# One load for K's weights, one load for each pair of last weight rows, and tile 3's transposes ahead of K2's second pass

## The chip, the cores and the metric

The program runs on one core of a Trainium2 chip. The metric is the device time of one execution in microseconds (us); a run's figure is the median of several executions. A separate execution was profiled, and its trace is what the views below are taken from.

## What is computed

The input `x` has 2048 rows (tokens) of 576 values. It is normalised, goes through a linear-attention block with 32 heads of 18 values and through a GEGLU feed-forward block of width 4608, and both results are added to `x`:

```python
xn  = layernorm(x)
q, k, v = split(xn @ wqkv)                 # wqkv: 576 x 1728, heads of 18
pq, pk  = phi(q), phi(k)                   # phi(t) = (t+1 if t>0 else exp(t)) + 1e-6
kv = sum_s pk[s] v[s]^T ;  z = sum_s pk[s]
A  = ((pq @ kv) / (pq . z + 1e-6)) @ wo
B  = (gelu(xn @ w_gate) * (xn @ w_up)) @ w_down
out = x + A + B                            # all inputs and the output in bf16
```

## The kernel before

**Tiling.** The 2048 tokens are 16 tiles of 128 (tile n holds every sixteenth token). The 576 columns are five contraction tiles: four of 128 and a last one of 64. To use all of TensorE's rows for the odd 64, a matrix product is done as "row tiles": each matmul uses only 64 of the 128 contraction rows, two run side by side on the two halves (`LO` = partitions 0 to 63, `HI` = 64 to 127), and each writes to a PSUM bank of its own. A product (`_Unit`, line 242) therefore has two passes. In the first (`rows`, line 258, often called p1 here) `LO` works for bank 0 and `HI` for bank 1; in the second (`p2`, line 271) they change places. Between them stands a "turn", a no-op on GpSimd (POOL) that makes the second pass wait for the first.

**The tokens of the head.** `_Token` (line 434) makes K or Q of one tile: its 576 output columns are two halves of 288, one for each bank. Its first pass has contraction tiles 0 to 3 (8 matmuls), its second has tiles 0 to 4 (10 matmuls). Contraction tile 4, the last 64 rows of the weights, is read from `w_ends`: one half of the columns lies in partitions 0 to 63 and the other half in 64 to 127, so that each half has the last rows where its second pass works.

**The weight loads.** `load_w_main` (line 167) brings rows 0 to 511 of K's or Q's weights, or some of its four contraction tiles. `load_w_ends` (line 172) brings the last 64 rows with two loads of 64 partitions x 576 bytes. The start of the kernel (lines 207 to 218) issues on SyncE's queue (SP): tile 0 of x, K's weights in two parts (contraction tiles 0 and 1, then 2 and 3, `W_PARTS`), tile 2 of x, Q's weights in two parts, tile 3 of x, and Q's ends. Tile 1 of x is issued by ScalarE (ACT), K's ends by POOL.

**What keeps TensorE (PE) busy before data is there.** `spin` (line 228) issues 31 matmuls of 128 x 128 on a tile `warm` that VectorE (DVE) sets to zero (line 210). `row_spin` issues eight more between the transposes of tile 0 and tile 1.

**Normalising.** Tiles 0 and 1 are handled as "centred" tiles: only the mean is subtracted before K and Q are computed, and the results are scaled afterwards. Tiles 2 and 3 are normalised first. Each of the four goes through PE transposes (line 358, PSUM banks from `tp_banks`, tile 3 in banks 2 and 3) and two copies to SBUF, one by ACT and one by DVE (line 363). Later tiles are transposed by DMA (line 366).

**The order.** The order on PE is written by hand (line 490):

```python
line = "t0 t1 K0a K0b K1 . . Q0a Q1a Q0b Q1b t2 u1 . . K2 Q2 . t3 . K3 Q3 .".split()
```

`t` and `u` are a tile's transposes, a name such as `K1` is its first pass, `K0a` and `K0b` are the halves of a first pass that go with the two parts of the weights, and a "." is the second pass of the oldest product that still lacks it. Thus `K2 Q2 . t3 . K3` reads: first passes of K2 and Q2, second pass of K2, transposes of tile 3, second pass of Q2, first pass of K3. After that the raw gate/up products (`g`) alternate with the other K tiles. The other engines' orders come from `in_order` (line 70), a planner that plays all steps with costs and ready times written into the code (`X_AT`, `W_AT`, `ready=`) and emits them in the order of its simulated starts. SP's later loads follow a fixed list (line 606). After the head come the Gram matrix of `xn` and `pk`, the attention state, the gate/up products in four blocks of 512 tokens, and the down products.

Of the kernel before, what the change touches and what calls it, by code (L numbers as in the profile page):

```python
# [10 lines left out]
BF16 = mybir.dt.bfloat16  # L11
F32 = mybir.dt.float32
PSUM = bass.MemoryType.PSUM

P = 128
HP = 64
S = 2048
D = 576
# [8 lines left out]
HALF = D // 2  # L27
# [5 lines left out]
EPS_LN = 1e-5  # L33
# [1 line left out]
GUB = 2  # L35
NB = NF // GUB
NWBUF = 4
NWARM = 31
XW = D + HP
RAW = 14  # L40
PK0 = 18
# [4 lines left out]
HEAD_T = RAW_T + ("Q2",)  # L46
LATER = 40.0
CENTRED = (0, 1)
W_PARTS = ((0, 1), (2, 3))
LEAD = 5  # L50


# [37 lines left out]
def kernel(  # L90
# [11 lines left out]
    nc = tc.nc  # L102
# [8 lines left out]
    const = ctx.enter_context(tc.tile_pool(name="const", bufs=1))  # L111
# [5 lines left out]
    ps_all = psum.tile([P, 8, 512], F32, name="ps_all")  # L117
# [4 lines left out]
    LO, HI = slice(0, HP), slice(HP, P)  # L122
# [7 lines left out]
    xnT = persist.tile([P, KT, S], BF16, name="xnT")  # L130
# [24 lines left out]
    wqkv_sb = apool.tile([P, KT, 3 * D], BF16, name="wqkv_sb")  # L155
    xn = apool.tile([P, NS, XW], BF16, name="xn")
    xcT = apool.tile([P, KT, len(CENTRED) * P], BF16, name="xcT")
    w_ends = apool.tile([P, 2, HALF], BF16, name="w_ends")
# [5 lines left out]
    def load_x(n0, cnt, on=nc.sync):  # L164
        on.dma_start(x_sb[:, n0:n0 + cnt, 0:D], x_view[:, n0:n0 + cnt, :])  # L165

    def load_w_main(which, kts=slice(0, 4)):
        c = slice(which * D, (which + 1) * D)
        view = A_wqkv[0:4 * P, c].rearrange("(kt p) c -> p kt c", p=P)
        nc.sync.dma_start(wqkv_sb[:, kts, c], view[:, kts, :])  # L170

    def load_w_ends(which, on):
        for i, rows in enumerate((HI, LO)):
            c = which * D + i * HALF
            on.dma_start(w_ends[rows, which, :], A_wqkv[512:576, c:c + HALF])

    def load_w_last(which, rows):
        c = slice(which * D, (which + 1) * D)
# [4 lines left out]
    def load_ends(i, on=nc.sync, parts=(0, 1)):  # L183
        c = slice(GUB * P * (i % NB), GUB * P * (i % NB + 2))
        if parts[0] == 0:
            wr_pairs[i // 2] = wr_bufs.next()
        for part in parts:
            on.dma_start(wr_pairs[i // 2][(LO, HI)[part], :], (B_w_gate, B_w_up)[part][512:576, c])

    def load_gu(i, part):  # L190

        if i >= NSC * NB:
            return
        f0 = GUB * (i % NB)
        c0, c1 = f0 * P, (f0 + GUB) * P
        if part == 0:
            gu_blocks[i] = (wg_bufs.next(), wu_bufs.next())
            if i % 2 == 0 and i:
                load_ends(i)
            nc.sync.dma_start(gu_blocks[i][0][:], B_w_gate[0:512, c0:c1].rearrange("(kt p) c -> p kt c", p=P))  # L200
        else:
            nc.sync.dma_start(gu_blocks[i][1][:], B_w_up[0:512, c0:c1].rearrange("(kt p) c -> p kt c", p=P))
# [3 lines left out]

    load_x(0, 1)
    nc.scalar.preload_act_table_set("natural_log_exp_and_others")
    warm = const.tile([P, P], BF16, name="warm")
    nc.vector.memset(warm[:], 0.0)  # L210
    nc.vector.memset(x_sb[:, 1, 0:1], 0.0)
    load_x(1, 1, nc.scalar)
    load_w_ends(1, nc.gpsimd)
    for which in (1, 0):
        for kts in W_PARTS:
            load_w_main(which, slice(kts[0], kts[-1] + 1))
        load_x(3 - which, 1)
    load_w_ends(0, nc.sync)

    act_bias = const.tile([P, 1], F32, name="act_bias")  # L220
    eps_ln = const.tile([P, 1], F32, name="eps_ln")
    nc.vector.memset(eps_ln[:], EPS_LN)
    ident = const.tile([P, P], BF16, name="ident")
    make_identity(nc, ident[:])
    bmask = const.tile([P, CR], F32, name="bmask")
# [2 lines left out]
    def spin(count):  # L228

        for _ in range(count):  # L230
            nc.tensor.matmul(ps_all[:, 7, 0:P], lhsT=warm[:], rhs=warm[:], start=True, stop=True)

    def row_spin(count):

# [3 lines left out]

    spin(NWARM)

# [125 lines left out]
        nc.sync.dma_start_transpose(xnT[:, :, n * P:(n + 1) * P], xn[:, n, :])  # L366

    X_AT = [3.46, 3.86, 6.40, 8.70]
    W_AT = {"K": (5.00, 5.70), "Q": (7.50, 8.50)}
    DMA_FREE = 8.9  # L370

    places = {}
# [11 lines left out]
    for n in range(NS):  # L384
# [26 lines left out]
        ready = [("rstd", n if n < 6 else both), twin]  # L411
# [3 lines left out]
        on, took = ("ACT", 0.92) if NORM[n] == "A" else ("DVE", 0.45)  # L415
# [18 lines left out]
    class _Token:  # L434

        def __init__(self, kind, n, ring=banks):
            self.kind, self.n, self.c = kind, n, (D if kind == "K" else 0)
            self.banks = two_banks(ring)
            self.unit = _Unit(
                [ps_all[:, b, :HALF] for b in self.banks], lambda i, rows, kt: (xcT if n in CENTRED else xnT)[rows, kt, n * P:(n + 1) * P],  # L440
                self.weights, nc.gpsimd, first=range(KT - 1), then=range(KT),
            )
            self.acc = ps_all[:, self.banks[0]:self.banks[0] + 2, :HALF]

        def weights(self, i, rows, kt):
            if kt == 4:
                return w_ends[rows, self.c // D, :]
            return wqkv_sb[rows, kt, self.c + i * HALF:self.c + (i + 1) * HALF]

        def raw(self):  # L450
            dst = (pk if self.kind == "K" else pq)[:, self.n, :].rearrange("p (h c) -> p h c", h=2)
# [35 lines left out]
                out=hT[:, self.f:self.f + NF + 1:NF, :], in_=ps_all[:, self.two[0]:self.two[0] + 2, :],  # L487
            )

    line = "t0 t1 K0a K0b K1 . . Q0a Q1a Q0b Q1b t2 u1 . . K2 Q2 . t3 . K3 Q3 .".split()  # L490
    follow = [f"g{i}" for i in range(LEAD)]
    for i in range(12):
        follow += [f"K{i + 4}"] + ([f"g{i + LEAD}"] if i + LEAD < RAW else [])
# [10 lines left out]
    def pe(name, took, after, call, ready=0.0):  # L504
        if name in steps:
            s = steps[name]
            s.after = s.after + ([pe_prev[0]] if pe_prev[0] else [])
        else:
            step(name, "PE", took, 0, after + ([pe_prev[0]] if pe_prev[0] else []), call, ready=ready, tail=0.17)
        pe_prev[0] = name  # L510
# [4 lines left out]
    for b in range(RAW // GUB):  # L515
        for part in range(2):
            war = [("p2", f"g{2 * (b - 4) + 1}")] if b > 4 else [("p2", "g1")] if b == 4 else []
            war += [(("gu", b, 0), "q")] if part else [(("gu", b - 1, 1), "q")] if b else []
            load(("gu", b, part), 0.6 + 1.1 * (b % 2 == 0 and part == 0 and b > 0), 262 + 131 * (b % 2 == 0 and part == 0 and b > 0), 6.8 + 6.0 * (b - 1), war,
                 lambda b=b, part=part: load_gu(b, part), ready=5.4, count=1 + 2 * (b % 2 == 0 and part == 0 and b > 0))  # L520

    def p2_step(u):
        n = int(u.name[1:])
# [16 lines left out]
    for name in line:  # L540
        if name == ".":
            p2_step(pending.pop(0))
            continue
        kind, n = name[0], int(name[1:].rstrip("ab"))
        if kind == "u":
            pe(("tu", n), 0, [], None)
            owner[(tp_banks[2], tp_banks[2] + 1)] += [("xnU", n, 0), ("xnU", n, 1)]
            continue
        if kind == "t":
            two = (tp_banks[n], tp_banks[n] + 1)  # L550
            steps[("tp", n)].after = steps[("tp", n)].after + owner.get(two, [])
            pe(("tp", n), 0, [], None)
            owner[two] = [("xnT", n, 0), ("xnT", n, 1)]
            if name == "t0":
                pe("spin", 0.22, [], lambda: row_spin(4))
            continue
        if name[-1] == "b":
            u = pending[-1 if name[:2] == pending[-1].name else -2]
            pe(("p1", u.name), 0.245, [], lambda u=u: u.p1(W_PARTS[1]), ready=W_AT[kind][1])
            step(("turn", u.name), "POOL", 0.06, clock, [("p1", u.name)], u.swap, tail=0.05)  # L560
            continue
        u = _Chain()
        u.name, u.at = name[:2] if name[-1] == "a" else name, clock
        if kind in "KQ":
            u.body = _Token(kind, n, head_banks if u.name in HEAD_T else banks)
            b = u.body.banks
            after = [("xnT", n)]
            t1, u.t2 = 0.49, 0.615
            u.p1 = u.body.unit.rows
            u.swap = u.body.unit.swap  # L570
            u.unit_p2 = u.body.unit.p2
            at = W_AT[kind][0 if name[-1] == "a" else -1]
        else:
            u.body = _Raw(n)
            b = u.body.two
            blk = n // GUB
            after = [("xnU" if m in CENTRED else "xnT", m) for m in range(TPC)] + [("gu", blk, i) for i in range(2)] + [("ends", 0), ("ends", 1)] * (blk == 0)
            t1, u.t2 = 1.08, 0.865
            u.p1 = u.body.rows
            u.swap = lambda body=u.body: body.unit.swap()  # L580
            u.unit_p2 = lambda body=u.body: body.unit.p2()
            at = 0.0
        after += owner.get(tuple(b), [])
        clock += t1 + u.t2
        if name[-1] == "a":
            pe(("p1a", u.name), 0.245, after, lambda u=u: u.p1(W_PARTS[0]), ready=at)
        else:
            pe(("p1", name), t1, after, u.p1, ready=at)
            step(("turn", name), "POOL", 0.06, u.at, [("p1", name)], u.swap, tail=0.05)
        pending.append(u)  # L590
# [372 lines left out]
    for sc in range(NSC):  # L963
# [15 lines left out]
        for j, t in enumerate(tiles):  # L979
            u = t.unit()  # L980
# [45 lines left out]
```

## Time and profile before

| | us |
|---|---|
| median of 3 runs | 506.54 (506.53 to 506.62) |
| the profiled execution's own time | 506.81 |
| span of its trace (first to last instruction) | 505.1 |
| PE busy | 500.3 (99%) |
| DVE, ACT, POOL busy | 230.1, 152.1, 10.5 |
| DMA queue q1 (all loads that SP issues) | 113802 packets, 60.54 MB |
| granted TensorE clock | 1.00 in every stretch |

How to read the views: the timeline lists, in order of time, the start, the length and the engine of merged instructions, and in brackets how long the engine stood idle before and what ended that. "PEld" is the load of the stationary operand, which overlaps the matmuls. An engine's name with a q ("SPq", "POOLq") is its queue while it issues a DMA. The chain of waits follows the work that ended last back to the start. In the list of DMA queues the columns are packets, MB, and the time that the packets took as a share of 16 DMA engines over the window asked for; q1 carries what SP issues, q10 what ACT issues, q0 what POOL issues.

Issues on SP at the start, from the timeline: x tile 0 at 0.81, the two parts of K's weights at 1.27 (0.93 us for both), x tile 2 at 2.24, the two parts of Q's weights at 2.75 (0.94), x tile 3 at 3.74, the two loads of Q's ends at 4.25 (1.26), the first gate load at 5.56.

### The profile page before, as it was taken

How to read it: one execution, taken by the hardware profiler on the slowest of the kernel's cores; microseconds unless marked ns; L12 is line 12 of the kernel's file. 1: busy time of each engine (PE TensorE's matmuls, PEld its weight loads, DVE VectorE, ACT ScalarE, POOL GpSimd, SP SyncE). 2: the span in 40 equal slices, each digit the busy share in tenths (PEclk: the TensorE clock that was granted, in tenths of full speed). 3: DMA queues.
4: the chain of work that ended last, by engine and by line, in shares of the span. 5: the costliest groups of instructions: out<-in, count | busy, mean ns of one | idle time of the engine just before them, and what ended most of it. 6: DMA issues, size and time to landing. Idle time of an engine off the chain costs nothing.

```text
span 505.1 us, 13641 instructions
## 1 busy us (share of the span) xinstructions
PE 500.3 (99%) x5976; PEld 375.3 (74%) x5976; DVE 230.1 (46%) x483; ACT 152.1 (30%) x265; POOL 10.5 (2%) x34
## 2 busy tenths in 40 slices
PE   8999999999999999999999999999999999999997
PEld 7666784568999666667999666667999666667994
DVE  5768996773002655553002665553002665553001
ACT  6778735432001422332001522332001432232000
POOL 3110100000000000000000000000000000000000
PEclk9999999999999999999999999999999999999999
DMA  9997917994112355665001455654001455640000
GB/s 225 273 221 161 310 48 216 272 227 109 31 55 65 108 161 172 164 150 109 13 14 54 117 152 170 172 154 108 14 13 47 126 150 162 164 119 14 13 14 23
DMA packets 114132, 61.74 MB, mean 122 GB/s; under 512 B 23954, under 2 KB 114010, under 8 KB 114074
## 3 DMA queue, kind: packets, MB, share of 16 engines
q1 hardware_dynamic: 113802, 60.54, 45.8%
q8 instruction: 46, 0.75, 0.7%
q0 software_dynamic: 128, 0.21, 0.2%
q10 hardware_dynamic: 144, 0.15, 0.1%
q14 instruction: 12, 0.10, 0.1%
HBM read 53.60 MB, written 2.36 MB: 111 GB/s over the span
## 4 chain that ended last, share of the span: by engine, by line
PE 98%; DMA 1%; SPq 0%; DVE 0%; issue 0%
PE ps_all L253 92%; PE ps_all L636 3%; PE ps_all L943 2%; DMA wqkv_sb<-in_A_wqkv_dram 1%; PE ps_all L644 0%; PE ps_all L663 0%; PE ps_all L948 0%; PE ps_all L358 0%; SPq L170 0%; SPq L165 0%; DVE res L957 0%; PE ps_all L682 0%; PE ps_all L936 0%
## 5 line engine op out<-in xcount | busy, mean ns | idle before, releaser
L253 PE MATMUL ps_all<-xnT,wg 64*128 64x512 bf16 x1152 | 276.3, 376 | 0.0
L253 PE MATMUL ps_all<-xnT,wu 64*128 64x512 bf16 x1152 | 271.5, 376 | 0.0
L253 PEld LDWEIGHTS <-wg 64*128 64x128 bf16 x1152 | 108.3, 94 | 49.9
L253 PEld LDWEIGHTS <-wu 64*128 64x128 bf16 x1152 | 108.3, 94 | 48.3
L833 DVE TENSOR_TENSOR hT<-ps_all,gl 128x512 bf16<-128x512 f32 x130 | 89.8, 691 | 105.3 <-ACT gl L832 104.9
L253 PEld LDWEIGHTS <-hT 64*128 64x128 bf16 x2160 | 132.6, 94 | 0.4
L832 ACT ACTIVATE gl<-ps_all 128x512 f32<-128x512 f32 x130 | 77.6, 597 | 155.2 <-PE ps_all L253 154.7
L957 DVE TENSOR_TENSOR res<-ps_all,x_sb 128x288 bf16<-128x288 f32 (+2 forms) x32 | 13.2, 452 | 143.1 <-PE ps_all L253 134.7
L253 PE MATMUL ps_all<-wd_a,hT 64*128 64x288 bf16 x960 | 64.9, 283 | 0.0
L253 PE MATMUL ps_all<-xnT,wr 64*128 64x512 bf16 x288 | 59.0, 376 | 0.0
L253 PE MATMUL ps_all<-hT 64*128 64x288 bf16 x720 | 50.2, 283 | 0.0
L854 ACT ACTIVATE gl<-ps_all 128x288 f32<-128x288 f32 x24 | 9.2, 409 | 122.9 <-PE ps_all L253 120.5
L253 PE MATMUL ps_all<-wd_m,hT 64*128 64x288 bf16 x480 | 35.5, 283 | 0.0
L253 PEld LDWEIGHTS <-xnT 64*128 64x128 bf16 x504 | 29.2, 94 | 4.0 <-ACT xnT L363 0.3
L253 PEld LDWEIGHTS <-wr 64*128 64x128 bf16 x288 | 18.4, 94 | 12.1
L253 PE MATMUL ps_all<-m_sb,pqT 64*128 64x288 bf16 x270 | 23.4, 283 | 0.0
L253 PE MATMUL ps_all<-wqkv_sb,xnT 64*128 64x288 bf16 x256 | 19.7, 283 | 0.0
L253 PEld LDWEIGHTS <-pqT 64*128 64x128 bf16 x270 | 17.0, 94 | 0.3
L636 PE MATMUL ps_all<-hT,xn 128*128 128x288 bf16 x128 | 16.0, 286 | 0.0
L486 ACT CAST hT<-ps_all 128x1024 bf16<-128x1024 f32 x14 | 14.1, 1010 | 4.9 <-PE ps_all L253 4.5
L636 PEld LDWEIGHTS <-xn 128*128 128x128 bf16 x128 | 12.4, 98 | 3.5 <-issue 0.5
L253 PE MATMUL ps_all<-wo,xnT 64*128 64x288 bf16 x216 | 13.8, 283 | 0.0
(104 smaller groups left out, 258.8 us busy)
## 6 DMA issues: line engine op xcount, KB each, us to landing
wg<-in_B_w_gate_dram SPq DMA_DIRECT2D x72, 256.0 KB, 3.1
wu<-in_B_w_up_dram SPq DMA_DIRECT2D x72, 256.0 KB, 3.6
wd_a<-in_B_w_down_dram SPq DMA_DIRECT2D x4, 576.0 KB, 9.4
wr<-in_B_w_gate_dram SPq DMA_DIRECT2D x35, 64.0 KB, 3.3
wr<-in_B_w_up_dram SPq DMA_DIRECT2D x35, 64.0 KB, 2.9
out_dram<-res SPq DMA_DIRECT2D x15, 144.0 KB, 1.8
x_sb<-in_A_x_dram SPq DMA_DIRECT2D x6, 288.0 KB, 5.1
hT<-in_B_w_down_dram SPq DMA_DIRECT2D x4, 432.0 KB, 5.5
```

The source lines that it names most:

```text
L253: return nc.tensor.matmul(self.outs[i], lhsT=self.lhs(i, rows, kt), rhs=self.rhs(i, rows, kt), start=start, stop=stop, skip_group_check=True,)
L486: nc.scalar.copy(out=hT[:, self.f:self.f + NF + 1:NF, :], in_=ps_all[:, self.two[0]:self.two[0] + 2, :],)
L636: nc.tensor.matmul(ps_all[:, two[hf], :HALF], lhsT=xn[:, n, kt * P:(kt + 1) * P], rhs=pk[:, n, hf * HALF:(hf + 1) * HALF], start=(n == gra ...
L832: nc.scalar.activation(out=gl[:], in_=ps_all[:, b[0], :], func=ACT.Gelu_apprx_tanh)
L833: nc.vector.tensor_tensor(out=hT[:, GUB * k + i, :], in0=ps_all[:, b[1], :], in1=gl[:], op=ALU.mult)
L854: nc.scalar.activation(out=e[:, :HALF], in_=acc, func=ACT.Exp)
L943: nc.tensor.matmul(self.acc(hf), lhsT=hT[:, f, self.cols], rhs=wd(f)[:, self.parts[hf]], start=False, stop=False, skip_group_check=True,)
L957: nc.vector.tensor_tensor(out=self.res[:, hs], in0=self.acc(hf), in1=x_sb[:, self.n, hs], op=ALU.add)
```

## The change

K's 512 main rows come in one load; Q's stay in two parts. K0's first pass is one step of 8 matmuls. The last 64 rows come in one load for K and one for Q, each into 128 partitions; this puts the first half of the columns into partitions 0 to 63 and the second half into 64 to 127, the other way round than before, so `_Token` swaps which bank and which half of the columns the two row halves serve. The spin uses a constant tile of ones that the program's opening has written already, and has 32 matmuls; the small constant `eps_ln` is set earlier. Tile 3's transposes stand ahead of K2's second pass. The planner is told that K's weights are ready at 5.70 and that the first gate/up loads may be issued from 4.9 on, not 5.4.

```diff
-NWARM = 31
+NWARM = 32
-W_PARTS = ((0, 1), (2, 3))
+WQ_PARTS = ((0, 1), (2, 3))
...
     def load_w_ends(which, on):
-        for i, rows in enumerate((HI, LO)):
-            c = which * D + i * HALF
-            on.dma_start(w_ends[rows, which, :], A_wqkv[512:576, c:c + HALF])
+        view = A_wqkv[512:576, which * D:(which + 1) * D].rearrange("r (i c) -> i r c", i=2)
+        on.dma_start(w_ends[:, which, :], view)
...
-    warm = const.tile([P, P], BF16, name="warm")
-    nc.vector.memset(warm[:], 0.0)
+    warm = nc.const_aps.tensor(1.0, [P, P], BF16)
+    eps_ln = const.tile([P, 1], F32, name="eps_ln")
+    nc.vector.memset(eps_ln[:], EPS_LN)
     nc.vector.memset(x_sb[:, 1, 0:1], 0.0)
     load_x(1, 1, nc.scalar)
     load_w_ends(1, nc.gpsimd)
-    for which in (1, 0):
-        for kts in W_PARTS:
-            load_w_main(which, slice(kts[0], kts[-1] + 1))
-        load_x(3 - which, 1)
+    load_w_main(1)
+    load_x(2, 1)
+    for kts in WQ_PARTS:
+        load_w_main(0, slice(kts[0], kts[-1] + 1))
+    load_x(3, 1)
     load_w_ends(0, nc.sync)
...
-    W_AT = {"K": (5.00, 5.70), "Q": (7.50, 8.50)}
+    W_AT = {"K": (5.70,), "Q": (7.50, 8.50)}
...
-                [ps_all[:, b, :HALF] for b in self.banks], lambda i, rows, kt: ...
+                [ps_all[:, b, :HALF] for b in reversed(self.banks)], lambda i, rows, kt: ...
...
-            return wqkv_sb[rows, kt, self.c + i * HALF:self.c + (i + 1) * HALF]
+            return wqkv_sb[rows, kt, self.c + (1 - i) * HALF:self.c + (2 - i) * HALF]
...
-    line = "t0 t1 K0a K0b K1 . . Q0a Q1a Q0b Q1b t2 u1 . . K2 Q2 . t3 . K3 Q3 .".split()
+    line = "t0 t1 K0 K1 . . Q0a Q1a Q0b Q1b t2 u1 . . K2 Q2 t3 . . K3 Q3 .".split()
...
-                 lambda b=b, part=part: load_gu(b, part), ready=5.4, count=...
+                 lambda b=b, part=part: load_gu(b, part), ready=4.9, count=...
```

## The prediction, made before the result was known

> **What bounds the kernel now.** The chain of waits, read first, is PE for 98%. Whatever shortens the kernel must start PE's unbroken stretch earlier or take an idle moment out of it. The chain holds one wait worth the name:
>
> ```profile
> 1.27 0.42 SPq L170
> ...
> 1.73 4.84 DMA wqkv_sb<-in_A_wqkv_dram
> 6.57 0.04 issue
> 6.62 3.12 PE ps_all L253 x48
> ```
>
> The second part of K's weights, issued at 1.73, lands at 6.57; from 6.62 PE's work is back to back. The timeline of the first 14 us shows what stands around that wait, and one more gap:
>
> ```profile
> 5.63 0.42 PE L253 MATMUL ps_all<-wqkv_sb,xcT 64*128 64x288 bf16 x4
> 6.62 1.40 PE L253 MATMUL ps_all<-wqkv_sb,xcT 64*128 64x288 bf16 x20 [0.57 <-DMA wqkv_sb<-in_A_wqkv_dram]
> 7.05 0.82 DVE L304 BATCH_NORM_STATS2 stats<-x_sb 128x6 f32<-128x288 bf16 x2 [1.02 <-DMA x_sb<-in_A_x_dram]
> ...
> 11.40 0.72 ACT L453 ACTIVATE pq<-ps_all,rstd 128x576 bf16<-128x576 f32 x1
> 12.66 0.32 PE L358 MATMUL ps_all<-ident,xn 64*128 64x64 bf16 x10
> 13.55 0.51 PEld L253 LDWEIGHTS <-xnT 64*128 64x128 bf16 x10 [0.26 <-ACT xnT L363]
> ```
>
> K0's first four matmuls run at 5.63, then PE waits 0.57. DVE too waits for a load, tile 2 of x (7.05). K3's first pass waits for tile 3's copies: the pair before it starts at 13.30 and a pair takes 0.12, so it could start at 13.42 and starts at 13.58: 0.16 idle. After that the list of waits has PE waiting for nothing.
>
> Why do the loads land when they do? From 2.5 us on the 16 DMA engines are full, as this stretch of the table by windows shows (its last columns: clock, DMA share, GB/s), so earlier issues alone cannot bring data earlier. The list of DMA queues over 0 to 5 us, and over 0 to 6 us, gives progress:
>
> ```profile
> 4.00:4.50 0.50, 0.50 (x8) 0.30 (x7) 0.50 (x2) 0.50 (x1) 0.11 (x1) 1.00 1.06 313
> ```
>
> ```profile
> q1 hardware_dynamic: 673, 0.72, 48.3%
> ```
>
> ```profile
> q0 software_dynamic: 64, 0.07, 4.0%
> ```
>
> A load of 128 rows is 144 packets (queue q10, one such load, shows 144): a row each and one small packet per engine. Tile 0 and K's weights are 144 + 272 + 272 = 688, reached in sum at 5.05. Tile 0 (144, reached at 3.0) landed at 3.31, the first part of K (416, at 4.0) at 4.67: 0.3 to 0.7 behind the sum. The second part is 1.5 behind, tile 2 (832, at 5.55; landed 7.05) 1.5, Q's second part (1376, at 7.2; 8.92) 1.7, tile 3 (1520, at 7.55; 9.44) 1.9. A load lands when its last engine is done; so from some 4.1 us on at least one of the 16 was about 1 us behind its fellows in this execution.
>
> **The change, part by part.**
>
> *K in one load.* V's 512 rows, loaded in one piece, took 0.57 to issue (45.32); K's parts took 0.93. SP is 0.36 ahead. The full engines hide that: nothing. Were they not full, 0.36 at most.
>
> *K0's first pass unsplit.* The 20 matmuls from 6.62 to 7.84 take 0.061 each; four take 0.245. They ran under the wait and now stand behind it: **+0.245** after the landing.
>
> *The ends in one load each.* This decides. The trace shows that a load doesn't always use 16 engines: between 76 and 80.45 us only the two loads of `wo` run (126 partitions of four rows, and 72 of one, 576 rows).
>
> ```profile
> DMA packets 602, 0.66 MB, mean 149 GB/s; under 512 B 26, under 2 KB 602, under 8 KB 602
> ```
>
> 26 small packets end them, 14 + 12 and not 32: the largest divisors up to 16 of 126 and of 72. In these loads both sides count the same outermost. The new ends don't: SBUF counts 128 partitions, the view "i r c" of DRAM counts 2 halves. If shares are counted off on both sides, two engines carry all 128 rows, 64 each; if by SBUF alone, 16. I take two: a share must be found on either side, and 2 is the largest number that divides both counts, as 14 does in the row above. The Trainium skill says the same ("DMA: Bandwidth & Descriptors", section "Why a DMA increments its semaphore by 16 and not by 1": the largest number up to 16 that divides the slowest dimension of both sides); by that rule it is two engines, and the trace agrees with its 14 and 12, but shows no load with unequal sides. The same page's "Rules for kernel authors" advises one load of 128 partitions for two of 64, which by itself would make this part cost nothing.
>
> Price of two: K's ends (q0) took 4.0% of 16 engines over 6 us, 3.84 us of engine time, 0.24 an engine. On two engines it is 1.92 each, 1.68 more. From the other side: an engine carries 313/16 = 19.6 to 376/16 = 23.5 GB/s (4.0 and 6.0 us), so 36.9 KB cost 1.57 to 1.88, less 0.24. I take 1.5 (1.3 to 1.7). Without this the loads would land about 0.55 behind the sum; with it 2.0. K: 5.05 + 2.0, less up to 0.5 where q0's last packets (first ones at 3.8 in the trace's q0 counts) come after K's: 6.8. Tile 2: 7.6 to 7.7 instead of 7.05, **+0.65**. Q's second part: 9.25 instead of 8.92. Tile 3: 9.6 instead of 9.44.
>
> PE after that: K0's whole first pass at 6.85, against 6.375 (6.62 less 0.245): +0.47. But tile 2 is later still: norms of tiles 2 and 1 end at 9.63 + 0.65 = 10.28, tile 1's second transposes start at 10.39 (a DVE result reaches PE in 0.11: 4.36 to 4.47), Q0's second pass at 10.53 instead of 9.84: +0.69. Q's second part is needed at Q0b, 9.06 + 0.47 = 9.53: it is there. Q's ends: in the trace SP's small rows move at 283 GB/s (8 to 9.5 us), 17.7 an engine, so 36.9 KB take 2.1 on two engines; they would land at 8.1 + 2.1 = 10.2 and are needed at 10.34 + 0.69 = 11.03.
>
> *Tile 3's transposes earlier.* They can't start before Q0's results have left banks 2 and 3 (ACT, 11.40 to 12.12) and tile 3 is normalised (DVE, 12.04). Both hang on tile 2 through the norms and DVE's order: 12.12 + 0.65 + 0.11 = 12.88, while PE arrives at 11.07 + 0.98 + 0.69 = 12.74. Transposes take 0.145 of PE's order (12.66 to 12.81), the two second passes 1.23 (20 x 0.061): K3 at 14.26 instead of 13.58, **+0.68**. The gap of 0.16 goes; a wait of 0.14 ahead of the transposes comes. If landings did not move, the same sum gives 12.12 + 0.11 + 0.145 + 1.23 = 13.61: the move alone is worth 0, because what ended the gap is late on the other side. It adds no DMA and is passed by no queue of SP or POOL; behind the waiting PE stand K2's and Q2's second passes, for which DVE and ACT wait.
>
> *The rest.* The spin loses its wait for DVE (starts at 1.06, `warm` written at 0.89; the constants at 0.38) and gains a matmul of 0.112; it ends at 4.55 as before within 0.1, and K's weights are 2 us away: 0. If that cover went, 0.1. POOL and SP each lose one issue of 0.6; the first gate load goes out 1 us earlier, behind everything above in the same queue, and is needed at 15.4: 0. The planner may order some step otherwise: 0, with 0.2 either way.
>
> Sum: 506.81 + 0.68 = 507.49. The median is 0.27 below the profiled execution, part of it presumably that engine that was behind, whose place the two engines now take. Half of 0.27 stays: **507.35**, 0.81 over the median (0.16%; a measurement of this kernel tells 0.2%, 1.0 us, from no change).
>
> **The rivals.**
>
> *16 engines after all* (0.28). Then K lands as before or, without a late engine, at 5.6; SP's shorter queue helps a little, K0 costs 0.245, the tile-3 floor makes it +0.05 on the profiled time at worst and up to 0.6 less at best. 506.4 (506.0 to 506.8). For it: every other load of the trace goes by its partitions. Against it: the row of 26 can't tell.
>
> *Slower: Q's ends come too late* (0.17). If both ends fall on the same two engines, these are 1.5 behind when they begin Q's 64 rows: landing at 8.1 + 1.5 + 2.1 = 11.7, Q0's second pass waits from 11.03, 0.67 more, of which the wait before tile 3 hides 0.14: K3 at +1.2, 507.9. It decides as soon as the ends land after 11.0. For it: the start of the row of engines is the obvious place for both. Against it: two queues, two ways of issuing.
>
> *The change doesn't bring K earlier*: that is in the forecast, since the bytes ahead of K's last row are the same.
>
> *Much faster* is excluded: all PE idle that could go is 0.57 + 0.16 = 0.73, under 0.2%.
>
> **How the numbers follow.** Forecast 0.52 (own range 506.9 to 507.8), 16 engines 0.28, late ends 0.17, something unnamed 0.03. Over 507.55: a third of the first (0.16), nearly all of the second rival (0.14), 0.02 of the rest: slower 0.32; faster 0.01; same 0.67. The range reaches over both rivals: 506.1 to 508.0.
>
> **What would show it.** Two engines: Q's ends lose 30 of their 32 small packets on q1 (16 of 32 with sixteen engines); K lands after 6.3, tile 2 after 7.4, and PE's one long wait is over 0.9. Sixteen: tile 2 lands by 7.0. Late ends: a PE wait for `w_ends` near 11. Tile 3: no wait at K3, one ahead of the transposes. I am wrong as a whole if x and K land earlier than 6 us and PE still gains nothing, or if PE waits after 15 us.

## The result, and the profile after

The changed kernel takes 507.52 us (median of 17 runs, 507.32 to 508.80) against 506.62 for the kernel before (17 runs, 506.19 to 508.40): ratio 1.0017, 95% interval 1.0009 to 1.0025, so 0.9 us slower. The forecast said 507.35 in a range of 506.1 to 508.0. The profiled execution's own time is 508.43, 2.6 over its span of 505.8, where before it was 1.7 over 505.1; the median span of the 17 runs is 505.8 too, so spans and times inside the trace are what can be compared. The changed file's lines count one lower (L252 for L253, L635 for L636).

The end of the chain of waits after (start, length, what), from its last wait on:

```profile
3.82 7.71 DMA w_ends<-in_A_wqkv_dram
...
11.56 1.89 PE ps_all L252 x28
13.46 0.15 PE ps_all L357 x10
13.60 43.86 PE ps_all L252 x524
57.46 11.87 PE ps_all L635 x96
```

Before, PE's unbroken stretch hung on K's second part. Now it hangs on Q's ends, issued at 3.82 and landed 7.71 later. The last piece, the start of the Gram matrices, is a good yardstick for the head: 57.46, where before it was 56.38. That is 1.1 later, though the span grew by 0.7 only. The rest lies behind the end of the whole chain, whose last instruction ends at 503.39 in a span of 505.8, and before at 502.32 in 505.1: 2.4 follow it instead of 2.8. SyncE waits there for the last store of the output, 0.7 now and 1.0 before. Why the store was quicker no run shows. The timeline of the same kernel shows the stops around it:

```profile
5.80 1.70 PE L252 MATMUL ps_all<-wqkv_sb,xcT 64*128 64x288 bf16 x24
...
7.83 0.30 PE L252 MATMUL ps_all<-w_ends,xcT 64*128 64x288 bf16 x2 [0.33 <-DMA w_ends<-in_A_wqkv_dram]
...
11.56 0.30 PE L252 MATMUL ps_all<-w_ends,xcT 64*128 64x288 bf16 x2 [0.82 <-DMA w_ends<-in_A_wqkv_dram]
...
13.28 0.33 PE L357 MATMUL ps_all<-ident,xn 64*128 64x64 bf16 x10
...
14.65 1.04 PE L252 MATMUL ps_all<-wqkv_sb,xnT 64*128 64x288 bf16 x14
```

```profile
6.45 0.82 DVE L303 BATCH_NORM_STATS2 stats<-x_sb 128x6 f32<-128x288 bf16 x2 [0.25 <-DMA x_sb<-in_A_x_dram]
...
9.74 0.82 DVE L303 BATCH_NORM_STATS2 stats<-x_sb 128x6 f32<-128x288 bf16 x2 [0.70 <-DMA x_sb<-in_A_x_dram]
```

The wait of 0.57 for K's weights is gone: K0's first pass starts at 5.80 and goes on. In its place stand two waits for `w_ends`: 0.33 for K's (7.83) and 0.82 for Q's (11.56). Tile 2 of x is there at 6.45, earlier than before, tile 3 at 9.74. Nothing waits at tile 3's transposes (13.28) or at K3 (14.65, before 13.58).

The list of DMA queues of the whole execution (packets, MB, share of 16 engines), and the same list over the first 5 us:

```profile
q1 hardware_dynamic: 113756, 60.54, 47.1%
...
q0 software_dynamic: 208, 0.21, 0.1%
```

```profile
q1 hardware_dynamic: 729, 0.80, 53.7%
...
q0 software_dynamic: 1, 0.00, 0.4%
```

q1 lost 46 packets of 113802: 16 because K's weights end once instead of twice, and 30 for Q's ends, two small packets instead of 32. That is the count announced for two engines. And POOL's queue, q0, has moved one packet by 5.0, where before it had moved 55.

### The profile page after: what moved, and what is told of

Read it like the earlier page. It is cut to its first block, busy times and chain, and to the rows that moved or that the text cites. A ratio compares the mean times of both kernels' runs of the same rounds, so it can differ in the third digit from the quotient of the medians.

```text
span 505.8 us, 13637 instructions
## 1 busy us (share of the span) xinstructions
PE 500.2 (99%) x5977; PEld 375.4 (74%) x5977; DVE 230.6 (46%) x482; ACT 152.2 (30%) x265; POOL 10.2 (2%) x33
## 4 chain that ended last, share of the span: by engine, by line
PE 97%; DMA 2%; SPq 1%; issue 0%; DVE 0%
PE ps_all L252 91%; PE ps_all L635 3%; PE ps_all L942 2%; DMA w_ends<-in_A_wqkv_dram 2%; PE ps_all L643 0%; SPq L165 0%; PE ps_all L662 0%; SPq L170 0%; PE ps_all L947 0%; DVE res L956 0%; PE ps_all L681 0%; PE ps_all L357 0%; PE ps_all L935 0%
## 5 line engine op out<-in xcount | busy, mean ns | idle before, releaser
L252 PE MATMUL ps_all<-xnT,wg 64*128 64x512 bf16 x1152 | 276.3, 376 | 0.0
L252 PE MATMUL ps_all<-xnT,wu 64*128 64x512 bf16 x1152 | 271.5, 376 | 0.0
L252 PEld LDWEIGHTS <-wg 64*128 64x128 bf16 x1152 | 108.3, 94 | 49.8
L252 PEld LDWEIGHTS <-wu 64*128 64x128 bf16 x1152 | 108.3, 94 | 48.2
L252 PEld LDWEIGHTS <-hT 64*128 64x128 bf16 x2160 | 132.6, 94 | 0.4
L252 PE MATMUL ps_all<-wd_a,hT 64*128 64x288 bf16 x960 | 64.9, 283 | 0.0
L252 PE MATMUL ps_all<-xnT,wr 64*128 64x512 bf16 x288 | 59.0, 376 | 0.0
L252 PE MATMUL ps_all<-hT 64*128 64x288 bf16 x720 | 50.2, 283 | 0.0
L252 PE MATMUL ps_all<-wd_m,hT 64*128 64x288 bf16 x480 | 35.5, 283 | 0.0
L252 PEld LDWEIGHTS <-xnT 64*128 64x128 bf16 x504 | 29.6, 94 | 3.4
L252 PEld LDWEIGHTS <-wr 64*128 64x128 bf16 x288 | 18.4, 94 | 12.1
L252 PE MATMUL ps_all<-m_sb,pqT 64*128 64x288 bf16 x270 | 23.4, 283 | 0.0
L252 PE MATMUL ps_all<-wqkv_sb,xnT 64*128 64x288 bf16 x256 | 19.8, 283 | 0.0
L252 PEld LDWEIGHTS <-pqT 64*128 64x128 bf16 x270 | 17.0, 94 | 0.3
L635 PE MATMUL ps_all<-hT,xn 128*128 128x288 bf16 x128 | 16.0, 286 | 0.0
L635 PEld LDWEIGHTS <-xn 128*128 128x128 bf16 x128 | 12.4, 98 | 3.5 <-issue 0.5
L252 PE MATMUL ps_all<-wo,xnT 64*128 64x288 bf16 x216 | 13.8, 283 | 0.0
```

What stands on the lines that cost most here:

```text
L252: return nc.tensor.matmul(self.outs[i], lhsT=self.lhs(i, rows, kt), rhs=self.rhs(i, rows, kt), start=start, stop=stop, skip_group_check=True,)
L635: nc.tensor.matmul(ps_all[:, two[hf], :HALF], lhsT=xn[:, n, kt * P:(kt + 1) * P], rhs=pk[:, n, hf * HALF:(hf + 1) * HALF], start=(n == gra ...
```

## The experiments

Theory: the loss is the ends on two engines, and the rest of the change is worth 0. Rivals: the loss comes from another part (K in one load, the order of the transposes); or from joining loads, or from POOL's queue, and not from the number of engines. Runs of one group shared a chip and the runs of the kernel before; its median span was 505.1 in the first group, 504.9 in the second and 504.8 in the third. Spans of several runs scatter less than times, so the median span is given too.

### Group 1: the ends and the rest, apart

**Ends as four loads.** The change with the ends alone undone:

```
-        view = A_wqkv[512:576, ...].rearrange("r (i c) -> i r c", i=2)
-        on.dma_start(w_ends[:, which, :], view)
+        for i, rows in enumerate((LO, HI)):
+            c = which * D + i * HALF
+            on.dma_start(w_ends[rows, which, :], A_wqkv[512:576, c:c + HALF])
```

> The changed kernel, with the ends again in two loads of 64 partitions each (first half of the columns into partitions 0 to 63); all else as changed. Theory (the ends' loads on two engines cost the time): PE's waits for the ends (0.33 at 7.83 and 0.82 at 11.56 in the changed kernel's trace) go, tile 3 lands about 1 us earlier than 9.74, K3's first pass starts at 13.1 to 13.6 instead of 14.65; 506.0 to 506.6. Rival (the unsplit first pass of K0 and the new place of tile 3's transposes cost it, the waits being only where the loss shows): K3 stays at 14.3 or later, 507.2 to 507.6.

Measured 506.36 (506.01 to 507.55, 11 runs), ratio 0.9989 (0.9979 to 0.9999), median span 504.4. Of its timeline the start of K0's first pass and of K3's:

```profile
5.68 1.69 PE L253 MATMUL ps_all<-wqkv_sb,xcT 64*128 64x288 bf16 x24
...
12.79 1.40 PE L253 MATMUL ps_all<-wqkv_sb,xnT 64*128 64x288 bf16 x20
```

No wait stands between them, K3 comes earlier than the 13.1 to 13.6 expected, and the Gram matrices start at 55.59. In median spans the ends cost 505.8 - 504.4 = 1.4, and the rest of the change gains 505.1 - 504.4 = 0.7. That the rest is worth 0 falls.

**Only the ends joined.** The kernel before with the new `load_w_ends`, and the order of the halves that goes with it; nothing else.

> The kernel before, with nothing but the ends joined into one load for K and one for Q (and the halves swapped to fit). Theory (two engines): both waits of PE for the ends appear, K3's first pass at 14.3 to 14.9, 507.3 to 507.7. Rival (the other parts of the change cost it): within 0.2 of the kernel before.

Measured 508.96 (507.86 to 510.27, 6 runs), ratio 1.0041 (1.0027 to 1.0055); higher than expected. The spans fall into two groups: 508.0, 507.9 and 508.0 with a granted clock of 0.997, and 506.4, 506.1 and 506.0 with 1.000. The second three are 0.9 to 1.3 over the kernel before; the profiled one is of the first three. Its timeline, then two rows of its table by windows (PE, PEld, DVE, ACT, POOL busy, clock, DMA share, GB/s):

```profile
7.92 2.58 PE L252 MATMUL ps_all<-wqkv_sb,xcT 64*128 64x288 bf16 x20 [1.73 <-DMA wqkv_sb<-in_A_wqkv_dram]
...
8.17 0.82 DVE L303 BATCH_NORM_STATS2 stats<-x_sb 128x6 f32<-128x288 bf16 x2 [2.01 <-DMA x_sb<-in_A_x_dram]
```

```profile
7.00:8.00 1.00, 0.08 (x2) 0.07 (x3) 0.00 (x0) 0.42 (x2) 0.00 (x0) 0.92 1.10 345
8.00:9.00 1.00, 1.00 (x10) 0.72 (x11) 0.82 (x2) 0.00 (x0) 0.24 (x1) 0.50 0.92 256
```

Here the step happens that the forecast described: K's second part lands at 7.88 and tile 2 at 8.17, where before it was 6.57 and 7.05. In the two traces of group 3 that also have these ends and K in two loads, tile 2 is late again (7.81 and 7.87), but K's second part lands at 6.43 in the one that waits for it. And a cost comes that nobody had priced: PE idles 1.73, and from about the end of that wait the clock stands at 0.50 until about 11.3, so that ten matmuls pass in a microsecond instead of 20.

**Only Q's ends as two loads** (K's in one, as changed), and **only K's ends as two loads** (Q's in one): `load_w_ends` with the loop above for one of the two.

> The changed kernel, with Q's ends in two loads of 64 partitions and K's ends still in one. Theory (the two loads' engines are the same two, and Q's 64 rows queue behind engines that K's ends made late): the wait of 0.33 at K0's second pass stays, the one of 0.82 at Q0's goes or falls under 0.2, tile 3 still lands at 9.5 to 9.8; K3 at 13.8 to 14.1, 506.7 to 507.0. Rival (Q's ends are late for their own length alone): K's ends in one load do no harm beyond 0.33, K3 at 13.5, 506.4.

> The changed kernel, with K's ends in two loads of 64 partitions and Q's ends still in one. Theory (64 rows take two engines about 2 us, but these are not late when they begin): Q's ends land near 10.3 instead of 11.53, PE waits 0 to 0.4 for them; no wait at K0's second pass; K3 at 13.3 to 13.7, 506.2 to 506.7. Rival (Q's ends are late for their own length alone): PE's wait for them stays above 0.6 and the time at 507.0 or more.

With K's ends in one load the time is 507.51 (506.85 to 508.42, 11 runs), ratio 1.0014 (1.0005 to 1.0023), median span 505.6: all but 0.2 of the loss is still there, against the expectation. With Q's ends in one load it is 506.23 (506.02 to 507.36, 11 runs), ratio 0.9992 (0.9984 to 1.0001), median span 504.5, 0.1 over the four loads. The timeline of the first, K's ends in one load:

```profile
8.23 0.30 PE L257 MATMUL ps_all<-w_ends,xcT 64*128 64x288 bf16 x2 [0.77 <-DMA w_ends<-in_A_wqkv_dram]
...
10.16 0.82 DVE L308 BATCH_NORM_STATS2 stats<-x_sb 128x6 f32<-128x288 bf16 x2 [0.91 <-DMA x_sb<-in_A_x_dram]
```

and of the second, Q's ends in one load, the matmuls that need them:

```profile
10.27 0.30 PE L257 MATMUL ps_all<-w_ends,xcT 64*128 64x288 bf16 x2
```

So the wait that the chain of the changed kernel names, 0.82 for Q's ends, is not the greater part of the cost. Take Q's two-engine load away, and K's ends are still late (0.77), DVE waits 0.91 for tile 3, and the median span is only 0.2 shorter. Take K's away, and Q's ends, which landed at 11.53, land at 10.23 and PE waits some 0.3 for them (the eight matmuls before start at 9.46 and take 0.49). This fits two loads that stood one behind the other on the same two engines; no view names the engines. The start of the Gram matrices in the single traces gives Q's ends a somewhat larger part: 55.59 with no ends joined, 56.17 with Q's, 56.98 with K's, 57.46 with both, so 0.5 to 0.6 for Q's and 1.3 to 1.4 for K's. Spans say less for Q's: of these four traces the two with Q's ends joined have an end of 2.4 behind the chain, the other two one of 2.8. K's ends are the greater part by either measure.

### Group 2: K's load, the transposes, the way of joining

All four start from the ends as four loads.

**Tile 3's transposes back in their old place**: `K2 Q2 . t3 . K3` in the line of the order.

> The changed kernel with the ends in four loads of 64 partitions, and tile 3's transposes back between K2's and Q2's second passes. With the four loads and the transposes early PE ran from 5.68 to K3's first pass at 12.79 without a wait. If the move is worth something, it is because the copies behind the transposes have K2's and Q2's 1.23 of cover instead of Q2's 0.62 alone: PE comes to the transposes at 11.42 + 0.62 = 12.04, their copies end 0.81 later as before (11.42 to 12.23), at 12.85, and K3 starts at 12.95 behind a wait of about 0.15: 506.5, 0.15 over the four loads. If the move is worth 0, as the forecast said, K3 stays at 12.8 and no wait stands ahead of it: 506.4.

Measured 506.35 (506.12 to 507.11, 12 runs), ratio 0.9990 (0.9980 to 1.0001), median span 504.6. In time it equals the transposes ahead (506.36), in span it is 0.2 longer on another chip; the move is worth 0 to 0.2. The trace has the first case of the two expected:

```profile
13.16 0.30 PE L253 MATMUL ps_all<-w_ends,xnT 64*128 64x288 bf16 x2
13.44 1.65 PE L253 MATMUL ps_all<-wqkv_sb,xnT 64*128 64x288 bf16 x24
```

The pair at 13.16 takes 0.12, so K3 could start at 13.28 and starts at 13.44: the wait of 0.16 of the kernel before is back. With the four loads and the transposes ahead it is gone and nothing waits in its place.

**K's weights in two loads again**, with K0's first pass split:

```
-    load_w_main(1)
+    for kts in WQ_PARTS:
+        load_w_main(1, slice(kts[0], kts[-1] + 1))
-    line = "t0 t1 K0 K1 ...
+    line = "t0 t1 K0a K0b K1 ...
```

> The changed kernel with the ends in four loads, and K's weights again in two loads with K0's first pass split in two. If K in one load is worth nothing, as the forecast said, K0's first pass still starts at 5.68 (tile 0's copies end then), goes on without a wait and K3 stays at 12.8: 506.4. If the second issue on SP makes K's last rows later, by the 0.36 that the forecast named or more, PE waits for K's weights inside K0's first pass and K3 starts at 13.1 to 13.6: 506.7 to 507.2.

Measured 506.92 (506.30 to 507.82, 12 runs), ratio 0.9998 (0.9988 to 1.0008), median span 504.9: as long as the kernel before, 0.3 over the run beside it (transposes back) and 0.5 over the four loads. The chain names the load:

```profile
1.73 4.45 DMA wqkv_sb<-in_A_wqkv_dram
```

K's second part lands at 6.18, while K's one load was there by 5.68, 5.76 and 5.88 in three runs with the ends in loads of 64 partitions. What also differs is when POOL's queue gets its turn. The list of queues over the first 5 us, K in two loads and, in the second fence, K in one (the run with the ends as four loads):

```profile
q0 software_dynamic: 61, 0.07, 5.5%
```

```profile
q0 software_dynamic: 29, 0.04, 2.0%
```

In the same kernels q0 had moved 34 packets and none by 4.5, though POOL issues at 1.33 in both. With K in one load, then, K's rows went ahead of its ends. That this is what brings K earlier is argued from these counts, and why the start of q0 hangs on the number of SP's loads no run shows. The gain itself is read from the median spans: this single trace (span 504.6) does not have it, since its first 24 matmuls on K's weights are over at 7.45, and with K in one load at 7.20, 7.70 and 7.66.

**The ends cut the other way**: two loads of 64 partitions, each with K's and Q's piece of one row half, both on POOL's queue.

```
+    for i, rows in enumerate((LO, HI)):
+        view = A_wqkv[512:576, 0:2 * D].rearrange("r (w i c) -> r w i c", w=2, i=2)
+        nc.gpsimd.dma_start(w_ends[rows, :, :], view[:, :, i, :])
```

> The changed kernel with the ends in two loads that are cut the other way: 64 partitions each, K's and Q's pieces of one row half together (64 rows of two pieces on both sides), both on POOL's queue at the start. If it is the halves as outermost count on DRAM's side that put a load on two engines, both loads go to all 16, K's ends are there at 7.2 and Q's long before 9.7, PE has no wait above 0.2 after 5.7 and K3 starts at 12.8 to 13.0: 506.2 to 506.5, like the four loads, with two issues less. If joining loads as such is what costs, or 37 KB more ahead of tile 2 do, tile 2 is over 0.4 later than 6.25 and K3 starts at 13.2 or later: over 506.7.

Measured 506.23 (505.82 to 507.50, 12 runs), ratio 0.9989 (0.9980 to 0.9999), median span 504.45. Two loads instead of four cost nothing when both sides count 64 rows outermost. K3 starts at 13.25 in its trace, later than the 12.8 to 13.0 expected: K's weights land at 5.88, and the first 24 matmuls take 1.74 instead of 1.52 (the last section says why). It and the ends as four loads are the versions that come out below both kernels, by 0.1% against the kernel before, with intervals that reach to 0.9999.

**K's ends in one load on SP's queue**, behind K's weights, Q's as two:

> The changed kernel with Q's ends as two loads, and K's ends in one load on SP's queue right behind K's weights instead of on POOL's. If two engines for 128 rows are what costs, whichever queue brings them, tile 2's rows stand behind them on these two: some 2.0 for the rows (Q's ends on SP's queue took 2.0 from 8.9 to 11.0 in the changed kernel) less 0.25 for a share of 16; tile 2 lands at 6.25 + 1.7 = 8.0 and K3 starts 14 or later: 507.5 to 508.2. If the cost lay in POOL's queue, whose larger packets alternate with the rows of SP's, they are ordinary rows on SP's queue, tile 2 lands by 6.8 and K3 starts at 12.8 to 13.3: 506.3 to 506.8.

Measured 507.61 (507.43 to 508.24, 12 runs), ratio 1.0015 (1.0006 to 1.0024), median span 505.7: as long as with K's ends on POOL's queue. Its list of queues and its timeline:

```profile
q1 hardware_dynamic: 113916, 60.61, 46.5%
```

```profile
7.67 0.66 PE L257 MATMUL ps_all<-wqkv_sb,xcT 64*128 64x288 bf16 x8 [0.27 <-POOLq L268]
...
7.59 0.82 DVE L308 BATCH_NORM_STATS2 stats<-x_sb 128x6 f32<-128x288 bf16 x2 [1.34 <-DMA x_sb<-in_A_x_dram]
...
14.09 0.91 PE L257 MATMUL ps_all<-wqkv_sb,xnT 64*128 64x288 bf16 x12
```

q1 has 113916 packets, 130 over the 113786 of the ends as four loads: 128 rows and two small packets. On SP's queue, then, the load goes to two engines. On POOL's queue it costs as much (507.51), though the count there does not tell the engines (last section). So the cost does not need POOL's queue. Tile 2 lands at 7.59, 1.3 later than with four loads (6.25) and not the 1.7 expected. It also reaches PE by a way that the forecast had not named: POOL, which passes K0's turn on (L268), waits for tile 2 from 5.17 to 7.60, and PE with it (0.27).

### Group 3: what PE's idle time does to its clock

**Only the ends joined, with PE kept busy in the wait for K**:

```
-            pe(("p1a", u.name), ..., lambda u=u: u.p1(W_PARTS[0]), ready=at)
+            pe(("p1a", u.name), ..., lambda u=u: [u.p1(W_PARTS[0]) for _ in range(6 if u.name == "K0" else 1)], ready=at)
```

> The kernel before with the ends joined, as in the run that joined them alone, and with K0's first four matmuls issued six times over (the first of them starts its bank anew each time, so the sums are the same), 1.2 more of PE's time inside the wait for K's second part. In the run that joined the ends alone PE idled 1.7 to 1.9 there, and its granted clock then stood at 0.50 for some 3.5. If that idle time drops the clock, it stays at 1.00 here, every run has a span of 506.0 to 506.4 like those runs of the earlier kernel whose clock was 1.00, and the time is 507.8 to 508.1. If the clock falls for another reason, some of the runs still span 507.9, with 0.50 in some windows behind 7.

> The kernel before with the ends joined, once more, beside the run with the filled wait: the same split is expected, about half of the runs with a clock of 0.997 and a span of 507.9 to 508.0, and half with 1.000 and 506.0 to 506.4; the median between 508.0 and 509.6, above that of the filled wait by up to 1.7.

With the filled wait 508.30 (508.10 to 508.50, 6 runs), ratio 1.0033 (1.0021 to 1.0046), all spans 506.3 to 506.7 at a clock of 1.000. Beside it the kernel with only the ends joined, once more: 508.21 (507.90 to 509.24, 5 runs), spans 506.1 to 507.5 with a median of 506.4, 1.6 over the kernel before, none with a clock of 0.997. The two do not tell the theories apart: on this chip the drop did not come back without the filling either. The second one's timeline says why it need not:

```profile
6.47 0.91 PE L252 MATMUL ps_all<-wqkv_sb,xcT 64*128 64x288 bf16 x12 [0.34 <-DMA wqkv_sb<-in_A_wqkv_dram]
7.95 0.67 PE L252 MATMUL ps_all<-wqkv_sb,xcT 64*128 64x288 bf16 x8 [0.57 <-POOLq L263]
```

The same program's wait for K was 1.73 in one execution and 0.34 in another; behind these shorter idle stretches the granted clock stayed at 1.00.

**Ends as four loads, 14 matmuls of the spin instead of 32** (`NWARM = 14`):

> The changed kernel with the ends in four loads, and 14 matmuls of the spin instead of 32: PE idles from some 2.4 to 4.45 ahead of tile 0's transposes, 2.0. If an idle stretch of that length halves the granted clock, windows between 4 and 8.5 show 0.50, K0's and K1's first and second passes take twice their 0.061 a matmul, K3's first pass starts 1.0 to 1.7 later than 12.79 and the time is 507.4 to 508.1. If the length of the idle stretch isn't what counts, the clock stays at 1.00 and the time at 506.4, as the forecast has it within 0.1 for a spin that no longer covers.

Measured 508.07 (507.00 to 508.35, 11 runs), ratio 1.0023 (1.0014 to 1.0032): 1.7 over the full spin (506.36, on another chip). The spans fall into two groups, 505.3 to 505.8 (5 runs) and 506.4 to 506.6 (6 runs); the trace is of the first, and none shows the second. Its table by windows, and in the second fence the same microsecond with 32 matmuls:

```profile
6.00:7.00 1.00, 1.00 (x12) 0.74 (x10) 0.95 (x4) 0.97 (x4) 0.24 (x1) 1.00 1.09 362
7.00:8.00 1.00, 1.00 (x12) 0.77 (x10) 0.49 (x2) 0.85 (x4) 0.00 (x0) 1.00 1.11 334
8.00:9.00 1.00, 1.00 (x21) 0.88 (x17) 1.00 (x3) 0.51 (x1) 0.71 (x2) 1.00 1.16 291
```

```profile
6.00:7.00 1.00, 1.00 (x20) 0.79 (x18) 0.82 (x3) 0.97 (x4) 0.24 (x1) 1.00 1.08 356
```

PE is busy all through both, but with the short spin it passes 12 matmuls in a microsecond until 8.0 and 21 after it, and with the long one 20 already at 6. The first 24 matmuls on K's weights take from 5.57 to 8.14 instead of from 5.68 to 7.20. The column of the granted clock, expected to show 0.50, stays at 1.00: the slow start is seen in the count of matmuls alone.

## Why the prediction was right, and where it was not

The number was near (507.35 for 507.52), and the decisive step, that the ends go to **two engines**, was right: q1 lost its 46 packets, the 130 of K's ends on SP's queue count the two small ones, and the same bytes, in loads whose two sides both count 64 rows outermost, cost nothing extra. That the sum came so near is luck. Its +0.68 stands for a tile 2 that lands 0.65 late, and tile 2 came 0.6 earlier than before. K3 moved by 1.07, and the span by 0.7 only because what follows the end of the chain was 0.4 shorter.

Of the signs announced for two engines the packet count came; K after 6.3, tile 2 after 7.4 and a PE wait over 0.9 did not (5.80, 6.45 and 0.82), and tile 2 by 7.0 was the sign of sixteen. The landings could not tell the two apart; the packet count and the later runs do.

- **"K lands at 6.8, tile 2 at 7.7"** failed: K was there by 5.80, tile 2 at 6.45. The estimate let q0 start at 3.8 as in the trace of before. With K in one load it starts at about 5.0, behind K's last rows. With K still in two loads tile 2 came late in all three traces (7.81 to 8.17) and K's second part in one (7.88): the step exists there, and with K in one load it is gone.
- **"K in one load: 0"** failed: by the run with K in two it gains 0.3 to 0.5 of median span. That q0's late start is the reason fits the counts and is not shown.
- **K's ends themselves** were timed nowhere. They were nobody's wait before; on two engines they come 0.33 to 0.77 too late for K0's second pass, and with them tile 3 comes later (DVE waits 0.70 to 0.91 for it, where with four loads it waits for nothing). In spans this, alone, is all but 0.2 of the loss (median span 505.6 of 505.8, from 504.4).
- **Q's ends** were priced well by themselves: forecast 10.2, measured 10.23 when K's ends are spread, though PE was ready for them at 9.95 there and not at 11.03. The rival "both ends on the same two engines" fits what was measured: forecast 11.7 with a wait of 0.67, measured 11.53 with 0.82, and K3 at 14.65 where that rival gave 13.58 + 1.2 = 14.78. It had a chance of 0.17 and deserved more. The Trainium skill ("DMA: Bandwidth & Descriptors", section "Why a DMA increments its semaphore by 16 and not by 1") says that a load issued by SP takes the lowest-numbered engines, and one issued by POOL takes a run of engines from a cursor that goes round; nothing here shows the numbers, but the 1.3 between 10.23 and 11.53 agrees with one place for both.
- Yet the rival's price was wrong too: it gave its wait 0.5 of time, and with the wait gone the time stays (507.51) and the median span falls by 0.2. Behind K's late ends stands a late tile 3.
- **Tile 3's transposes: 0** held within 0.2, but not for its reason. It said that what ended the gap would be late on the other side; the gap of 0.16 is gone without a wait in its place, and comes back when the transposes go back. The wait forecast ahead of the transposes did not come, because what was late there was PE.
- **The spin: 0** was not tested by itself. "If that cover went, 0.1" was far off: 18 matmuls less cost 1.7, because the spin isn't only cover: with 14 matmuls PE ran at half its rate until 8.0.

In median spans: the change without the ends -0.7 (K in one load 0.3 to 0.5 of it, the transposes up to 0.2; the new spin and the planner's times have no run of their own), K's ends +1.2, Q's ends behind them +0.2, together +0.7, which is 505.1 to 505.8.

## What to carry to other kernels

Before joining two loads, count the outermost dimension on both sides: a destination of 128 partitions does not help a source that is seen as two halves; cut the loads so that the rows are outermost on both. A wait that the chain names is only the last of several; test it alone before calling it the cost, because here its removal left the time as it was and took 0.2 off the span, of the 1.4 that both joined loads cost. And a load that nobody waits for has a landing time too: when its engines or its turn change, write that time down against the instruction that needs it.

## What the runs showed of the hardware that was not expected

- PE starts at half its rate and changes to full at a moment that differs between executions. With 32 spin matmuls that was at about 3.8 in the changed kernel (an estimate: its spin takes 3.27, and 3.57 in the traces where all of it runs at half rate), by 6.0 in the ends as four loads, and at about 6.7 with the transposes back. So K0's first pass differs by some 0.4 between single traces of kernels that are equal up to there, and small differences in K3's start are not to be read from one trace. After the short spin it came 3.65 after PE resumed work (4.35 to 8.0). The Trainium skill ("TensorE: Matmul & The Clock Gate", section "Part 1: The HAM clock gate") gives about 3.4 us of work in a window that runs freely; the 3.65 agrees, and with the full spin the change came 3.0 to 5.8 after PE's first matmul, so not after a fixed time. It also says that an idle window of about 3.4 us brings the half rate back; the one trace with a drop shows it after an idle wait of 1.73, about half of that, and lasting 0.16 + 3.00 + 0.26 = 3.4 us. That this idle time was its cause is argued, not shown: it came in 3 of 6 runs on one chip, and in none of 5 on another.
- POOL's load, issued at the same time, begins later when SP issues K's weights as one load: by 5.0 it has moved 24 to 32 packets where K's ends are in loads of 64 partitions, against 55 and 61 with K in two loads, and 0 and 1 where they are one load, against 81 to 103. Why is open.
- On POOL's queue the load on two engines counts more packets, not fewer: without K's ends q0 shows 64 (K's ends on SP's queue), with them as two loads 128, and with them in one load 208. So the one load counts 144 and the two count 64, for the same bytes; SP's queue has 130 for the same load. The small packets that SP's queue saves POOL's doesn't, so on q0 their number does not tell the engines.
